# Wide chunks of an attention and feed-forward kernel: three operands of the second layer are built one product earlier, one scaling moves from GpSimd to VectorE, and GpSimd's sums wait

## The chip, the cores and the metric

The kernel runs on one core of a Trainium2 chip. The metric is the device time of one execution in microseconds (us). A core has TensorE (PE in the profile, with its weight loads as PEld), VectorE (DVE), ScalarE (ACT), GpSimd (POOL) and SyncE (SP, which issues DMAs).

## The reference

What is computed, cut to what matters:

```python
kv = np.einsum('bhsd,bhse->bhde', k, v)              # q, k, v: 8 x 8 x 576 x 64
out = np.einsum('bhsd,bhde->bhse', q, kv)
rms = np.sqrt(np.mean(out * out, axis=-1, keepdims=True) + 1e-06)
x = (out / rms * g_norm)                             # as 4608 tokens x 512
h = x @ w_in                                         # w_in: 512 x 2048
g = 0.5 * h * (1.0 + erf(h / sqrt(2)))
y = g @ w_out                                        # w_out: 2048 x 512
```

All arrays are 32-bit floats. A float operand of a matmul is kept as two parts: a high part (the value cast to a shorter type, `fp32r`) and a low part (the value less its high part), and three matmuls, high by high, low by high and high by low, stand for one.

## The kernel before

The tokens are worked in seven chunks. Chunks 0 and 1 (512 tokens each) are plain. Chunks 2 to 6 are wide, with 704, 704, 736, 736 and 704 tokens, and use a Strassen-like scheme: each 2 by 2 block product is made by seven products instead of eight. `FAST` is 2, the first wide chunk, and `NCH` is 7.

**Layer 1 of a wide chunk** is 28 products, `u` = 0 to 27, in four groups of seven (`m` = `u // 7`). Within a group the products come in the order `ORDER = (0, 2, 4, 6, 1, 3, 5)` and write the PSUM bank pairs X, Z, X, Z, Y, Z, Y. A product is 12 matmuls. After each, `Fast.behind` evacuates its bank pair: for product `k` = 0 ScalarE copies (L1205), for 4 ScalarE applies the gelu (L1196), and for 2, 6, 1, 3 and 5 VectorE adds the bank pair to a buffer `e` (L604), after which, for 1, 3 and 5, ScalarE applies the gelu. The bank pair of the last group's product 22 is written again by product 24, that of 24 by 26, and that of 25 by 27, so each of these VectorE adds has to end before the next product but one starts.

**Layer 2** is another 28 products of 12 matmuls ("ticks", table `TICKS`, which begins (0,0), (0,1), (0,2), (2,0), (2,1), (0,3)). An operand of it is made by `Fast.ready`, in two steps: `high`, a cast on ScalarE (L1254), and `low`, a subtraction on VectorE (L1258) that reads two SBUF operands. Operands (0,0), (0,1) and (0,2) are made while layer 1 goes on. Operand (0,3) needs the gelu of product 23; (2,0) and (2,1) need only blocks that were finished long before. Two sums of finished blocks (`Fast.combine`, L1241) run on GpSimd at products 24 and 25 of the last group.

**The next chunk's attention output** is prepared in `within`, beside the products of this chunk. For each of four head pairs `p`, `scale` makes a row of reciprocal norms by a transposition on VectorE (L361) and multiplies it in (L357, two SBUF operands), at products 15, 16, 18 and 20. Then `add_blocks` (L474) forms four sums T3, T1, T2 and T4, all of them on GpSimd.

A chunk without a next one (chunk 6) has neither scalings nor these four sums. In the kernel before, chunk 2 is a special case twice: only there VectorE multiplies the fourth pair (elsewhere GpSimd does), and only there the four sums stand at products 22 to 25 and the first, T3, waits for the `low` of operand (0,2), by `behind(op, latest["low"])`; elsewhere they stand at products 21 to 24 and T3 waits for its inputs alone.

Each engine takes its instructions in the order in which the code issues them; nothing reorders them. In the code, `layer.behind(m, k)` issues the evacuation of the product that was just issued, `within(c, u)` comes after it, and `layer.ready(...)` stood at the end of the loop's body.

Of the kernel before, what the change touches and what calls it, by code (L numbers as in the profile page):

```python
# [23 lines left out]
FAST = PLAIN  # L24
# [15 lines left out]
def linear_attn_rms_gelu_ffn(  # L40
# [18 lines left out]
    nc = tc.nc  # L59
# [3 lines left out]
    B, NP = kv_main.shape[:2]  # L63
# [28 lines left out]
    def pair_of_banks(pool, name):  # L92
        banks[name] = pool.tile([P, 2, 512], F32, name=f"banks_{name}")
# [32 lines left out]
    def block_tile(name, dtype):  # L126
        if name not in home:
            raise KeyError(name)
        width = 2 * WIDEST if name[0] == "d" else 2 * DM
        return home[name].tile([P, width], dtype, name=name)  # L130

    kv_in, late, latest = {}, {}, {}
# [7 lines left out]
    def load_keys(b, p):  # L140

        names["kv", p], t = take()
        main, tail = t[:, :2 * DM], t[:TAIL, 2 * DM:2 * DM + 2 * P]
        nc.sync.dma_start(out=main, in_=kv_main[b, p])
        nc.sync.dma_start(out=tail, in_=kv_tail[b, :, p])
        main, tail = (x.rearrange("p (a n) -> p a n", a=2) for x in (main[:KROWS], tail))
        parts = [main[:, :, j * P:(j + 1) * P] for j in range(NJ)] + [tail]
        kv_in[b, p] = [(x[:, 0], x[:, 1]) for x in parts]
# [409 lines left out]
    GROUPS = NF // 4  # L558
# [155 lines left out]
    def store(acc, t0, to):  # L714
        for t, ps in enumerate(acc):
            nc.scalar.copy(out=to[t], in_=ps)
            nc.sync.dma_start(out=out[t0 + t * P:t0 + (t + 1) * P, :], in_=to[t])
# [143 lines left out]
    for half in range(2):  # L861
# [6 lines left out]
        n = 2 + half  # L868
# [99 lines left out]
    def behind(op, other):  # L968

        tc.add_manual_dep(  # L970
            op.ins, other.ins.name,
            mybir.DependencyInfo(mybir.DependencyClass.Sync, mybir.DependencyReason.DATA),
        )
# [39 lines left out]
    def send():  # L1013

        for x in sent:
            product_out(*x)
        sent.clear()
# [54 lines left out]
    def second_layer(*slots):  # L1072
        c, i = divmod(slots[0], NF)
        if i == 0:
            acc[c] = [bank(f"acc{t}") for t in range(CH // P)]
        layer2(acc[c], [(g.pop(s), s % NF) for s in slots])

    for s in range(PLAIN * NF):
        c, i = divmod(s, NF)
# [43 lines left out]
        else:  # L1123
            spread_matmuls(c, i)
            g[s] = gelu(h.pop(s))
            nxt, k = attn[c + 1], SQUARES.index(i) if i in SQUARES else None
# [184 lines left out]
    def sum_keys(b, ps):  # L1311
        kv_ps[b, 0] = ps
        sum_kv(b, range(NP), ps)
        free.extend(names.pop(("kv", p)) for p in range(NP) if ("kv", p) in names)
        place_kv(b, range(NP))
# [1 line left out]
    SLOTS = 7 * GROUPS  # L1317
    KEYS, QUERIES, DEEPEN = (25, 32, 39, 45), (49, 53), (9, 11)
    SUM, VISITS, NORM = 1, (4, 8), (12, 13)
    SCALE, COMBINE, PIECES = (15, 16, 18, 20), (21, 22, 23, 24), range(31, 52, 3)  # L1320

    def visit(c, u):


        nxt, (a, b) = attn[c + 1], ("ZX" if c == FAST else "WX") if u == VISITS[0] else "WY"
        p = 2 * VISITS.index(u)
        nxt.project_pair(p, a)
        nxt.project_pair(p + 1, b)
        squares.append((p + 1, nxt.square(p + 1)))
        squares.append((p, a))  # L1330

    def within(c, u):

        if c + 3 < B and u in KEYS:
            load_keys(c + 3, KEYS.index(u))
        if c + 2 < NCH and u in QUERIES:
            attn[c + 2].load(QUERIES.index(u))
        if c + 1 == NCH:
            return
        nxt = attn[c + 1]  # L1340
        if c == FAST and u == 0:
            nxt.load(1)
        if c > FAST and u == SUM:
            sum_keys(c + 2, banks["W"][:, 1])
        if c == FAST and u == 2:
            sum_keys(c + 2, banks["Z"][:, 0])
        if u - 1 in VISITS:
            nxt.reduce(*squares.pop(0))
            p, a = squares.pop()
            squares.append((p, nxt.square(p, "w")))  # L1350
        if u - 3 in VISITS:
            nxt.reduce(*squares.pop())
        if u == NORM[0]:
            sums[c] = nxt.fold()
        if u == NORM[1]:
            nxt.inv = nxt.rsqrt(sums.pop(c))
        if u in SCALE:
            p = SCALE.index(u)
            eng = nc.vector if (c, p) == (FAST, NP - 1) else nc.gpsimd
            nxt.scale(p, eng, ("sq", "w")[p % 2])  # L1360
        late = u - (c == FAST)
        if late in COMBINE:
            k = COMBINE.index(late)
            op = nxt.add_blocks(("T3", "T1", "T2", "T4")[k], nc.gpsimd)
            if c == FAST and not k:
                behind(op, latest["low"])
        if u in PIECES:
            nxt.piece(ORDER[PIECES.index(u)])
# [4 lines left out]
    def sum_late(j, place):  # L1373
        names["sums", j], t = take()
        sum_out(j, (place, t[:, :2 * DM]), nc.gpsimd)

    def split_late(u):
        if u in LATE_SPLITS:
            j, h = LATE_SPLITS[u]
            name, t = take(F32R)  # L1380
            at = u if h else u + 1
            lows[at] = high_half(j, h, t[:, :2 * DM])
            split.append((at + 2, name, ("sums", j) if h else None))
        if u in lows:
            low_half(*lows.pop(u))
        if split and split[0][0] == u:
            _, name, whole = split.pop(0)
            for x in sent[:2]:
                product_out(*x)
            del sent[:2]  # L1390
            free.append(name)
            if whole:
                free.append(names.pop(whole))
# [6 lines left out]
    for c in range(FAST, NCH):  # L1400
        layer = Fast(c)
        for u in range(SLOTS):
            m, n = divmod(u, len(ORDER))
            k = ORDER[n]
            layer.product(m, k)
            if (c, u) == (FAST, 1):
                send()
                second_layer(*sorted(g))
                rows_out = [block_tile(n, F32) for n in SPARE[1:]]
                store(acc.pop(c - 1), (c - 1) * CH, [x[:, z * DM:(z + 1) * DM] for x in rows_out for z in range(2)])  # L1410
                acc_banks.release()
                more_banks = tc.alloc_tile_pool(name="more_banks", bufs=1, space=PSUM, reuse_waits="tile")
                for name in "YZ":
                    pair_of_banks(more_banks, name)
            if c + 1 < NCH and u in VISITS:
                visit(c, u)
            layer.behind(m, k)
            if c == FAST and u < 3:
                for j in ((6,), (1, 3), (5,))[u]:
                    attn[c].piece(j)  # L1420
            if c == FAST and u in (3, 6):
                sum_late(*((NJ2 - 2, "x0") if u == 3 else (NJ2 - 1, "x4")))
            within(c, u)
            if c == FAST:
                split_late(u)
            if c == FAST and u in DEEPEN:
                deepen()
            if (c, u) == (FAST, 6):
                low.release()
                last_room = tc.alloc_tile_pool(name="last_room", bufs=1, reuse_waits="tile")  # L1430
                home |= {n: last_room for n in LATE_ROOM}
                free += LATE_ROOM
            if n == 6 and m < GROUPS - 1:
                layer.high(0, m)
            if n == 0 and m:
                layer.low(0, m - 1)
            if n in (3, 4) and m:
                layer.combine((6, 2)[n - 3], m - 1, nc.gpsimd)
            if m == GROUPS - 1 and n > 3:
                layer.ready(*((0, 3), (2, 0), (2, 1))[n - 4])  # L1440
        for k in (6, 2):
            layer.combine(k, GROUPS - 1)
        for i, (k, n) in enumerate(TICKS):
            if i + layer.AHEAD < len(TICKS):
                layer.ready(*TICKS[i + layer.AHEAD])
            if 5 <= i < 5 + GROUPS:
                layer.combine(3, i - 5)
            if 9 <= i < 9 + GROUPS:
                layer.combine(1, i - 9)
            if c < NCH - 1 or i < len(TICKS) - GROUPS:  # L1450
                layer.matmuls(k, n)
                layer.after(k, n)
            within(c, SLOTS + i)
            if c == FAST:
                split_late(SLOTS + i)
        if c == NCH - 1:
            for side in range(2):
                for k, n in TICKS[-GROUPS:]:
                    layer.matmuls(k, n, (side,))
                    layer.after(k, n, (side,))  # L1460
# [61 lines left out]
```

## Time and profile before

| what | us |
| --- | --- |
| three runs: median, lowest, highest | 742.12, 740.96, 743.08 |
| the profiled execution: its own time | 741.02 |
| its span, first to last instruction | 739.2 |
| busy: PE, DVE, ACT, POOL | 732.6, 528.1, 357.3, 122.6 |

The span is 1.8 us shorter than the profiled execution's own time. Rows of the timeline give the start, the duration, the engine, the line of the code, the operation, output and input with sizes, and in brackets how long the engine stood idle just before and what ended that. The duration of a matmul group ends when its last result is modelled to be out, so consecutive groups overlap by 0.16 us; the distance from one start to the next is the time that a product takes. "busy" counts an instruction that is held up after its start as busy.

### The profile page before, as it was taken

The numbers are of one execution on the slowest core, as the hardware profiler recorded it, in microseconds if no ns is written. First come the engines' busy times: TensorE is split into PE (matmuls) and PEld (weight loads), VectorE is DVE, ScalarE is ACT, GpSimd is POOL, SyncE is SP. The second block draws the span as 40 slices with busy tenths as digits, with TensorE's granted clock in tenths as the row PEclk, the third lists the DMA queues.
The fourth block names the chain that finished last, engine by engine and source line by source line (L and its number), as shares of the span: only waits on it lengthen the run. The fifth ranks groups of instructions, "written<-read, shape, count | busy, mean of one in ns | idle before, by whom it ended". The sixth has DMA issues, their size and how long they took to land.

```text
span 739.2 us, 13288 instructions
## 1 busy us (share of the span) xinstructions
PE 732.6 (99%) x5150; PEld 696.3 (94%) x5150; DVE 528.1 (71%) x756; ACT 357.3 (48%) x565; POOL 122.6 (17%) x88
## 2 busy tenths in 40 slices
PE   8999999999999999999999999999999999999998
PEld 6888888888899999999999999999999999999997
DVE  3999998999857689357599257598257598254773
ACT  3788845643465367054365154365154364133640
POOL 1000000000045800013800014600015600022000
PEclk9999999999999999999999999999999999999999
DMA  9998985689998999988999978999978889988893
GB/s 343 407 408 284 364 283 200 220 313 359 346 335 314 361 336 387 408 317 282 323 325 371 406 243 271 313 326 361 395 230 281 276 291 310 335 295 289 295 318 121
DMA packets 84962, 233.66 MB, mean 316 GB/s; under 512 B 8484, under 2 KB 29476, under 8 KB 84900
## 3 DMA queue, kind: packets, MB, share of 16 engines
q1 hardware_dynamic: 84896, 232.82, 88.6%
q8 instruction: 41, 0.67, 0.4%
q14 instruction: 21, 0.17, 0.1%
q10 hardware_dynamic: 4, 0.00, 0.0%
HBM read 193.99 MB, written 38.80 MB: 315 GB/s over the span
## 4 chain that ended last, share of the span: by engine, by line
PE 93%; DMA 3%; DVE 1%; ACT 1%; issue 1%; ACTq 0%; DVEq 0%
PE banks_Z L1276 15%; PE banks_Z L1184 14%; PE acc L708 11%; PE h L676 10%; PE banks_X L1184 10%; PE banks_Y L1184 10%; PE banks_X L1276 10%; PE banks_Y L1276 9%; DMA w_out<-kv_main 1%; DMA w_in<-w_in 1%; PE banks_W L198 1%; PE banks_W L1184 1%; PE banks_W L414 1%; PE a L198 1%; PE banks_W L1276 0%
## 5 line engine op out<-in xcount | busy, mean ns | idle before, releaser
L1258 DVE TENSOR_TENSOR d<-d,d 128x704 fp32r<-128x704 f32 (+1 forms) x140 | 135.3, 988 | 33.8 <-ACT d L1254 33.6
L1254 ACT CAST d<-d 128x704 fp32r<-128x704 f32 (+1 forms) x140 | 105.0, 787 | 25.2 <-DVE d L1241 19.1
L604 DVE TENSOR_TENSOR e<-banks_Z,e 128x704 f32<-128x704 f32 (+1 forms) x53 | 47.7, 900 | 58.3 <-PE banks_Z L1184 46.8
L676 PE MATMUL h<-x,w_in 128*128 128x512 f32 x360 | 82.9, 380 | 0.0
L1276 PE MATMUL banks_X<-d,w_in 128*128 128x352 f32 (+1 forms) x504 | 79.1, 315 | 0.0
L1184 PE MATMUL banks_Z<-d,w_in 128*128 128x352 f32 (+1 forms) x468 | 78.0, 316 | 0.0
L676 PEld LDWEIGHTS h<-x,w_in 128*128 128x128 f32 x360 | 67.8, 189 | 10.1 <-ACT z L631 0.3
L708 PE MATMUL acc<-w_out,gh 128*128 128x512 f32 x256 | 77.0, 382 | 0.1
L1276 PEld LDWEIGHTS banks_X<-d,w_in 128*128 128x128 f32 x504 | 77.1, 189 | 0.0
L1184 PEld LDWEIGHTS banks_Z<-d,w_in 128*128 128x128 f32 x468 | 72.2, 189 | 1.1 <-DVE e L604 0.8
L1241 POOL TENSOR_TENSOR d<-d,d 128x704 f32<-128x704 f32 (+1 forms) x15 | 25.8, 1718 | 284.9 <-ACT d L1196 284.9
L1276 PE MATMUL banks_Y<-d,w_in 128*128 128x352 f32 (+1 forms) x432 | 67.2, 315 | 0.0
L1276 PEld LDWEIGHTS banks_Y<-d,w_in 128*128 128x128 f32 x432 | 66.1, 189 | 0.0
L1184 PE MATMUL banks_X<-d,w_in 128*128 128x352 f32 (+1 forms) x372 | 62.2, 317 | 0.0
L1184 PE MATMUL banks_Y<-d,w_in 128*128 128x352 f32 (+1 forms) x372 | 61.5, 315 | 0.0
L604 DVE TENSOR_TENSOR e<-banks_Y,e 128x704 f32<-128x704 f32 (+1 forms) x30 | 27.0, 903 | 47.4 <-PE banks_Y L1276 28.9
L1276 PE MATMUL banks_Z<-d,d 128*128 128x352 f32 (+1 forms) x360 | 59.8, 315 | 0.1
L1184 PEld LDWEIGHTS banks_X<-d,w_in 128*128 128x128 f32 x372 | 57.4, 189 | 1.4 <-issue 1.0
L1276 PE MATMUL banks_Z<-d,w_in 128*128 128x352 f32 (+1 forms) x360 | 57.9, 315 | 0.0
L1184 PEld LDWEIGHTS banks_Y<-d,w_in 128*128 128x128 f32 x372 | 57.6, 189 | 0.0
L1276 PEld LDWEIGHTS banks_Z<-d,d 128*128 128x128 f32 x360 | 55.8, 189 | 0.4 <-DVE d L1258 0.4
L708 PEld LDWEIGHTS acc<-w_out,gh 128*128 128x128 f32 x256 | 47.9, 189 | 8.5 <-issue 1.4
(228 smaller groups left out, 1129.7 us busy)
## 6 DMA issues: line engine op xcount, KB each, us to landing
w_in<-products_out SPq DMA_DIRECT2D x110, 512.0 KB, 4.8
w_in<-products_in SPq DMA_DIRECT2D x104, 512.0 KB, 4.8
d<-products_in SPq DMA_DIRECT2D x36, 512.0 KB, 5.1
d<-products_out SPq DMA_DIRECT2D x30, 512.0 KB, 4.6
products_in<-w_in SPq DMA_DIRECT2D x36, 256.0 KB, 5.2
w_in<-w_in SPq DMA_DIRECT2D x16, 512.0 KB, 10.2
w_out<-w_out SPq DMA_DIRECT2D x16, 512.0 KB, 10.2
products_out<-w_out SPq DMA_DIRECT2D x32, 256.0 KB, 5.3
```

What stands on the lines that cost most here:

```text
L198: nc.tensor.matmul(out=ps[r, n * D:(n + 1) * D], lhsT=k[:, r], rhs=v[:, r], start=(j == 0), stop=(j == NJ),)
L414: nc.tensor.matmul(out=to[rows(h), :, at], lhsT=kv[b % 2][rows(half), p, h ^ half], rhs=q[rows(half), h, :, at], start=True, stop=True,)
L604: return eng.tensor_tensor(out=out, in0=x, in1=y, op=op)
L676: nc.tensor.matmul(out=h, lhsT=parts["in", i][:, w][:, p * P:(p + 1) * P], rhs=woven(at.x[p][:, x]), start=(m + p == 0), stop=(m == 2 and ...
L708: nc.tensor.matmul(out=ps, lhsT=x[:, ts], rhs=woven(parts["out", i][:, w]), start=(i == 0 and m == 0), stop=(m == 2 and i == NF - 1),)
L1184: nc.tensor.matmul(out=ps[:, n], lhsT=y, rhs=woven(x[:, z, kb]), start=k in (0, 2, 1) and kb + i == 0, stop=kb == 1 and i == 2, skip_group ...
L1241: eng.tensor_tensor(out=out, in0=x, in1=y, op=op)
L1254: nc.scalar.copy(out=t[:, 0], in_=self.source(k, n))
L1258: latest["low"] = nc.vector.tensor_tensor(out=t[:, 1], in0=src, in1=t[:, 0].bitcast(F32), op=ALU.subtract)
L1276: nc.tensor.matmul(out=self.last(k, a) if alone else ps[:, a], lhsT=y, rhs=woven(x[:, z, p]), start=(alone or k in (0, 2, 1)) and n + p + ...
```

## The change

Three edits, in wide chunks:

- `layer.ready` for operands (0,3), (2,0) and (2,1) moves from the end of the loop's body at products 25, 26 and 27 to a place ahead of `layer.behind` at products 24, 25 and 26.
- The fourth pair is multiplied by VectorE in every wide chunk, not only in chunk 2.
- The four sums T3, T1, T2, T4 stand at products 22 to 25 in every wide chunk, and T3 waits for the latest `low` in every one.

```diff
-    SCALE, COMBINE, PIECES = (15, 16, 18, 20), (21, 22, 23, 24), range(31, 52, 3)
+    SCALE, COMBINE, PIECES = (15, 16, 18, 20), (22, 23, 24, 25), range(31, 52, 3)
...
-            eng = nc.vector if (c, p) == (FAST, NP - 1) else nc.gpsimd
+            eng = nc.vector if p == NP - 1 else nc.gpsimd
             nxt.scale(p, eng, ("sq", "w")[p % 2])
-        late = u - (c == FAST)
-        if late in COMBINE:
-            k = COMBINE.index(late)
+        if u in COMBINE:
+            k = COMBINE.index(u)
             op = nxt.add_blocks(("T3", "T1", "T2", "T4")[k], nc.gpsimd)
-            if c == FAST and not k:
+            if not k:
                 behind(op, latest["low"])
...
                 visit(c, u)
+            if m == GROUPS - 1 and 3 <= n < 6:
+                layer.ready(*((0, 3), (2, 0), (2, 1))[n - 3])
             layer.behind(m, k)
...
-            if m == GROUPS - 1 and n > 3:
-                layer.ready(*((0, 3), (2, 0), (2, 1))[n - 4])
```

On VectorE, chunk 3, from the last multiplication's row of norms to the end of layer 1 (`e` and `banks` are evacuations, L1258 the `low` of operands (0,2), (0,3), (2,0) and (2,1) in this order, each with the buffer `d` that it fills):

```order
 L361 STREAM_TRANSPOSE w<-y 128x736
+L357 TENSOR_TENSOR o<-o,w 128x736
 L1258 TENSOR_TENSOR d_3926<-d_3851,d_3926 128x704
-L604 TENSOR_TENSOR e_3959<-banks_Z,e_3941 128x704
-L604 TENSOR_TENSOR e_3993<-banks_Z,e_3941 128x704
-L604 TENSOR_TENSOR e_4011<-banks_Y,e_3993 128x704
-L1258 TENSOR_TENSOR d_4018<-d_3975,d_4018 128x704
+L604 TENSOR_TENSOR e_3957<-banks_Z,e_3941 128x704
+L1258 TENSOR_TENSOR d_3991<-d_3974,d_3991 128x704
+L604 TENSOR_TENSOR e_3994<-banks_Z,e_3941 128x704
+L1258 TENSOR_TENSOR d_4012<-d_3568,d_4012 128x704
+L604 TENSOR_TENSOR e_4015<-banks_Y,e_3994 128x704
```

The first two evacuations of the last group that are to be freed for products 26 and 27 (those of products 24 and 25) now have a `low` ahead of each; before, both came ahead of any of the three. In chunk 2 the same rows moved, but the multiplication (L357) stood there already.

On GpSimd, chunk 3, from the third pair's multiplication to the second block sum (L474 are T3, T1, T2 and T4, L1241 the block sums):

```order
 L357 TENSOR_TENSOR o<-o,sq 128x736
 L1241 TENSOR_TENSOR d_3715<-d_3715 128x704
-L357 TENSOR_TENSOR o<-o,w 128x736
 L474 TENSOR_TENSOR z<-o 128x736
 L474 TENSOR_TENSOR o<-o 128x2x368
 L474 TENSOR_TENSOR w<-z,o 128x736
+L1241 TENSOR_TENSOR d_3851<-d_3852,d_3851 128x704
 L474 TENSOR_TENSOR z<-o,w 128x736
-L1241 TENSOR_TENSOR d_3851<-d_3852,d_3851 128x704
 L1241 TENSOR_TENSOR d_3851<-d_3851 128x704
```

One instruction left GpSimd, and the first block sum now comes ahead of T4, as it did in chunk 2 before.

On ScalarE, chunk 3, the last group (L1196 are gelus, L1254 the casts of operands (0,3), (2,0) and (2,1)):

```order
 L1205 COPY e_3941<-banks_X 128x704
-L1196 ACTIVATE d_3975<-banks_X 128x704
-L1196 ACTIVATE d_3976<-e_4011 128x704
-L1254 CAST d_4018<-d_3975 128x704
+L1196 ACTIVATE d_3974<-banks_X 128x704
+L1254 CAST d_3991<-d_3974 128x704
+L1254 CAST d_4012<-d_3568 128x704
+L1196 ACTIVATE d_3975<-e_4015 128x704
```

The casts of (0,3) and (2,0) now follow the gelu of product 23 at once, ahead of the gelu of product 25.

## Rows read from the trace of the kernel before

**Rows 1.** The page, part 1: TensorE's busy time, share, instructions.

```profile
PE 732.6 (99%) x5150; PEld 696.3 (94%) x5150; DVE 528.1 (71%) x756; ACT 357.3 (48%) x565; POOL 122.6 (17%) x88
```

**Rows 2.** Waits of TensorE's weight loads, 199 to 739: total us, times, longest.

```profile
PEld banks_Z L1184 <- DVE e L604: 0.8, 2, 0.4
PEld banks_Z L1276 <- DVE d L1258: 0.4, 1, 0.4
```

**Rows 3.** Windows, products 24 to 27: length, busy PE, PEld, DVE, ACT, POOL, clock, DMA.

```profile
250.16:257.32 7.16, 7.16 (x50) 7.16 (x49) 2.74 (x3) 2.22 (x3) 7.08 (x6) 1.00 0.92 311
356.46:363.73 7.27, 7.27 (x50) 7.27 (x49) 2.75 (x3) 2.22 (x3) 7.11 (x5) 1.00 0.89 310
464.96:472.44 7.48, 7.48 (x51) 7.48 (x49) 2.89 (x3) 2.30 (x3) 7.32 (x5) 1.00 0.93 299
575.45:582.93 7.48, 7.48 (x51) 7.48 (x50) 2.89 (x3) 2.30 (x3) 7.25 (x6) 1.00 0.89 290
678.25:685.41 7.16, 7.16 (x51) 7.16 (x50) 2.75 (x4) 2.22 (x3) 0.86 (x1) 1.00 0.90 298
```

**Rows 4.** Timeline, chunk 2, last group of layer 1.

```profile
247.55 0.88 DVE L1258 TENSOR_TENSOR d<-d,d 128x704 fp32r<-128x704 f32 x1
248.58 1.68 POOL L474 TENSOR_TENSOR z<-o 128x704 f32<-128x704 f32 x1 [1.95 <-DVE d L1258]
250.34 1.69 POOL L474 TENSOR_TENSOR o<-o 128x704 f32<-128x704 f32 x1
250.43 0.76 ACT L1196 ACTIVATE d<-banks_X 128x704 f32<-128x704 f32 x1 [2.42 <-PE banks_X L1184]
251.98 1.69 POOL L474 TENSOR_TENSOR w<-z,o 128x704 f32<-128x704 f32 x1
253.74 1.95 PE L1184 MATMUL banks_Z<-d,w_in 128*128 128x352 f32 x12
256.36 1.35 DVE L1258 TENSOR_TENSOR d<-d,d 128x704 fp32r<-128x704 f32 x1 [1.52 <-ACT d L1254]
256.92 2.35 POOL L1241 TENSOR_TENSOR d<-d 128x704 f32<-128x704 f32 x1
```

**Rows 5.** Timeline, chunk 3, last group of layer 1 and a tick.

```profile
351.45 1.70 POOL L1241 TENSOR_TENSOR d<-d 128x704 f32<-128x704 f32 x1
352.86 0.77 ACT L1254 CAST d<-d 128x704 fp32r<-128x704 f32 x1
353.09 1.77 POOL L357 TENSOR_TENSOR o<-o,w 128x736 f32<-128x736 f32 x1
353.66 1.95 DVE L1258 TENSOR_TENSOR d<-d,d 128x704 fp32r<-128x704 f32 x1 [0.65 <-ACT d L1254]
355.53 0.88 DVE L604 TENSOR_TENSOR e<-banks_Z,e 128x704 f32<-128x704 f32 x1
356.46 2.06 PE L1184 MATMUL banks_Z<-d,d 128*128 128x352 f32 x12
356.64 0.76 ACT L1196 ACTIVATE d<-banks_X 128x704 f32<-128x704 f32 x1 [2.36 <-PE banks_X L1184]
370.89 2.32 PE L1276 MATMUL banks_Z<-d,d 128*128 128x352 f32 x12
```

**Rows 6.** Timeline, chunk 4: a transposition, the gelu of 23, an evacuation.

```profile
460.39 0.94 DVE L361 STREAM_TRANSPOSE w<-y 128x736 f32<-128x736 f32 x1
465.16 0.78 ACT L1196 ACTIVATE d<-banks_X 128x736 f32<-128x736 f32 x1 [2.49 <-PE banks_X L1184]
467.03 0.93 DVE L604 TENSOR_TENSOR e<-banks_Z,e 128x736 f32<-128x736 f32 x1 [2.25 <-PE banks_Z L1184]
```

**Rows 7.** Timeline, chunk 5: a transposition and the gelu of 23.

```profile
570.88 0.90 DVE L361 STREAM_TRANSPOSE w<-y 128x704 f32<-128x704 f32 x1
575.65 0.78 ACT L1196 ACTIVATE d<-banks_X 128x736 f32<-128x736 f32 x1 [2.49 <-PE banks_X L1184]
```

**Rows 8.** Timeline, chunk 6: the gelu of 23.

```profile
678.45 0.76 ACT L1196 ACTIVATE d<-banks_X 128x704 f32<-128x704 f32 x1 [2.36 <-PE banks_X L1184]
```

## The prediction

> **What bounds the kernel now.** I read the page's busy times first. TensorE is busy for 732.6 of 739.2 us [rows 1], so time is lost or won only where TensorE's products start later or sooner. Next I read whom its queue waits for in the wide chunks: in 540 us it waits 0.8 us, in two waits, for an evacuation that frees bank pair Z, and 0.4 us, once, for the `low` of a layer 2 operand [rows 2]. So no more than about 1 us is to be had here at all, and the question is whether the change makes new waits.
>
> The windows over products 24 to 27 show where to look. A product takes 7.16 / 4 = 1.79 us in the chunks of 704 tokens and 7.48 / 4 = 1.87 us in those of 736; chunk 3 alone took longer, 7.27. VectorE is busy only 2.7 to 2.9 us there. But GpSimd is busy for 7.1 to 7.3 us in chunks 2 to 5, all of the window, and for 0.86 in chunk 6 [rows 3]. In this window, with GpSimd at work without a pause, the three moved operands now fall.
>
> **What a `low` costs beside GpSimd.** A `low` takes 0.88 us when GpSimd is idle (247.55) [rows 4]. In chunk 3 one starts at 353.66 while GpSimd multiplies until 354.86; it ends at 355.61, 0.75 us after GpSimd has ended [rows 5]. Then GpSimd is held: in chunk 2 a `low` ends at 257.71, and the block sum that GpSimd had begun at 256.92, after the `low`, ends at 259.27, 1.56 us later [rows 4]. So a two-operand instruction of VectorE and one of GpSimd exclude each other: who began first finishes, and the other follows with 0.75 us (VectorE) or 1.56 us (GpSimd; scaled by 736/704, 1.63, an estimate). An evacuation, with one operand in PSUM, is not held: the one at 467.03 took its 0.93 [rows 6] beside GpSimd's busy window.
>
> **What an evacuation may cost.** A product can be read 0.20 us after the next one starts: in chunk 6 product 24 starts at 678.25, where the window begins [rows 3], and the gelu of 23 at 678.45 [rows 8]. The product after the next needs the bank pair back. So the add of 24 has 1.79 - 0.20 = 1.59 us for 0.89 us of work, and 0.65 us of slack after 0.05 us for the signal. Chunk 3 shows the price of missing it: with its gelu of 23 at 356.64, product 24 was due at 356.44; the evacuation of 22 ended at 356.41, the product started at 356.46 and took 2.06 us [rows 5] against the usual 1.95 [rows 4]. I count 0.10 for each restart.
>
> **The change, step by step.** With `ready` moved, VectorE's order is: `low` (0,3), evacuation of 24, `low` (2,0), evacuation of 25, `low` (2,1), evacuations of 26 and 27. The first `low` is ready when the gelu of 23 and a cast (0.77 in chunk 3 [rows 5], 0.80 in the wider chunks, the same by size) are done; I take 0.04 us between them and 0.03 us to VectorE, the latter as from 352.86 + 0.77 to 353.66 [rows 5]. The 0.04 no row shows; its bounds are -0.1 (no gap) and 0.08 (GpSimd's T3 to T1, 250.26 to 250.34 [rows 4]), and I take what lies between. A following VectorE instruction starts 0.08 us before the end of the one ahead (355.53 against 355.61).
>
> *Chunk 2.* The gelu ends at 251.19, the `low` is ready at 252.03. GpSimd's T2 begins at 251.98 [rows 4], 0.05 earlier. So T2 runs to 253.67, the `low` to 254.42, the evacuation of 24 to 255.23, and product 26, due at 253.74 [rows 4], starts at 255.28: 1.54 late, 1.64 with the restart. GpSimd's next sum is held to 255.98, so `low` (2,0) ends at 256.73, the evacuation of 25 at 257.54, and product 27, due at 255.28 + 1.89 = 257.17, starts at 257.59: 0.42, with the restart 0.52. Together **2.16 us**. Had the `low` come first: evacuation of 24 at 253.72 in time, T2 to 254.47, `low` (2,0) to 255.22, evacuation of 25 to 256.03, product 27 0.55 + 0.10 late: 0.65.
>
> *Chunk 3.* VectorE now multiplies the fourth pair; it is held by the block sum that ends at 353.15 [rows 5], ends at 353.90, and `low` (0,2), alone, at 354.70. T3 follows 0.15 us behind (248.43 to 248.58 in chunk 2 [rows 4]), and T1 ends two GpSimd sums later, at 354.85 + 1.77 + 0.08 + 1.77 = 358.47. `low` (0,3) is ready at 356.64 + 0.76 + 0.04 + 0.77 + 0.03 = 358.24, ahead of T2. It ends at 359.22, the evacuation of 24 at 360.02; product 26, due at 360.02, starts at 360.07: 0.15 with the restart. T2 to 360.85, `low` (2,0) to 361.60, evacuation of 25 to 362.40, product 27 at 362.45 instead of 361.96: 0.59. Together **0.74**.
>
> *Chunk 4.* Transposition to 461.33 [rows 6], multiplication (0.93, taken as the evacuation's [rows 6]) to 462.30, `low` (0,2) to 463.14, T1 to 466.9, T2 from 466.85. `low` (0,3) is ready at 465.16 + 0.78 [rows 6] + 0.04 + 0.80 + 0.03 = 466.81, 0.04 us before. By the same chain product 26 is in time and 27 loses **0.46**; had T2 come first, 1.66 + 0.51 = 2.17.
>
> *Chunk 5.* Its next chunk is narrower, so GpSimd's sums are shorter: transposition to 571.78 [rows 7], `low` (0,2) to 573.55, T1 to 577.16, T2 from 577.11 to 578.80. `low` (0,3) is ready at 575.65 + 0.78 + 0.87 = 577.30 [rows 7], 0.19 too late: it ends at 579.55, the evacuation of 24 at 580.40, product 26 at 580.45 instead of 579.19 (1.36), and 27 loses another 0.51. Together **1.87**.
>
> *Chunk 6.* GpSimd is idle [rows 3]; `low` (0,3) is ready at 678.45 + 1.60 = 680.05 [rows 8] and ends at 680.93, the evacuation of 24 at 681.74, 0.09 before product 26: **0**.
>
> *Gains.* The late evacuation of product 22 in chunk 3 goes, since the `low` ahead of it is no longer held by GpSimd's multiplication: 0.13. The tick at 370.89, 0.36 us too long [rows 5], goes too. `low` (2,1) and the evacuations of 26 and 27 come 2 us or more before the ticks that need them, so nothing follows there. Together -0.49. The multiplication on VectorE costs nothing by itself: VectorE is idle for more than half of the time [rows 3], and without that cover its 0.9 us would add to the next evacuation. T4 and GpSimd's second block sum, which operand (2,2) waits for, end about where they did, with one instruction less ahead of them and two more holds of 0.75; the tick of (2,2) is six products, over 10 us, behind product 27. The order of the DMAs is the same.
>
> **The sum.** 2.16 + 0.74 + 0.46 + 1.87 - 0.49 = +4.7 us. Against the profiled execution's own 741.0 that is 745.7; the median of the runs shown is 1.1 us above that execution, so 746.8.
>
> **A rule beside it.** The Trainium skill, page "SBUF — State Buffer", section "Who interferes with whom", says that "Issue order, not op shape, decides who blocks." The handover at 256.36 and 256.92 agrees with it [rows 4]. By the rule chunk 2 costs 2.16, and if a waiting VectorE were always let in first, 0.65; no row here has two starts as near as 0.05 us.
>
> **Rivals.** *The first `low` gets in ahead of T2 everywhere.* For it: margins of 0.05, 0.04 and 0.19 us against an unshown 0.04. Against: chunk 5 needs more than the bound of -0.1 gives. Chunks 2 to 5 then lose 0.65, 0.74, 0.46 and some 0.46, less 0.49: +1.8, 743.9. *T2 comes first in chunk 4 too:* 1.71 more, 748.5. *Not slower:* the `low` holds up no evacuation beyond its slack. This is decided by `low` (2,0): it has to end 0.36 to 0.55 us sooner than above in each of chunks 2 to 5, which it does if it doesn't wait for a whole GpSimd sum behind `low` (0,3). For it: VectorE is idle for over half of the window. Against: GpSimd is not [rows 3], and with its next sum always waiting behind a `low`, the next `low` meets it. Then only the gains stay: 741.6.
>
> **How the numbers follow.** What a measurement of this kernel can tell from no change is 0.3%, 2.2 us. The forecast with its neighbours (one of the near ties more or less) has 0.64, all of it slower; the first rival's 743.9 has 0.14, mostly within 0.3%; not slower 0.16, of which faster 0.03 (more than 2.2 us would need gains that no row shows); a loss of more than 7 us 0.06. So faster 0.03, same 0.25, slower 0.72. The range reaches from 743.3, 0.6 below the first rival, to 749.0, 0.5 above the second, for the scatter of the runs.
>
> **What would show it.** In the changed kernel's timeline: `low` (0,3) and (2,0) of 1.6 to 2.4 us in chunks 2 to 5 and 0.9 in chunk 6; waits of TensorE for VectorE's evacuations, about 1.4 us before product 26 in chunks 2 and 5 and about 0.5 us before product 27 in four chunks; windows of products 24 to 27 longer by 0.4 to 2.2 us; the tick of (2,1) in chunk 3 at 1.79. I am wrong if these `low`s run at 0.9, if the gelu of 23 or its cast is ready earlier than I have it, or if GpSimd's sums start later and leave the window free.

## The result

The changed kernel takes 747.61 us (median of six runs, 745.56 to 749.08) against 741.65 us for the kernel before in the same six rounds: a ratio of 1.0081, 95% interval 1.0067 to 1.0095, so 0.8% slower. Its profiled execution took 745.97 us with a span of 744.0 us, 4.8 us more than the span before. One execution of the first experiment below ran at a mean granted clock of 0.655 and took 1096.7 us; it counts in that run's median but not in its ratio.

The page, part 1, of the changed kernel:

```profile
PE 734.2 (99%) x5150; PEld 696.3 (94%) x5150; DVE 532.7 (72%) x759; ACT 358.1 (48%) x565; POOL 119.9 (16%) x85
```

Read beside [rows 1], TensorE's work is as it was (the weight loads are busy for the same 696.3 us), and its share still reads 99%. Of the 4.8 us, only 1.6 show there, as busy time of its matmuls (734.2 us for 732.6). The 4.8 us are found in the waits of its weight loads from 199 to 746 us (total us, times, longest):

```profile
PEld banks_Z L1184 <- DVE e L604: 4.0, 5, 1.6
PEld banks_Y L1184 <- DVE e L604: 2.1, 4, 0.6
```

Before, it was 0.8 for bank pair Z, nothing for Y, and 0.4 for a layer 2 operand [rows 2]. That last wait is gone. What was added is all for evacuations (L604) by VectorE. The windows over products 24 to 27 of chunks 2 to 6, with length and busy times in the columns of [rows 3]:

```profile
250.06:259.35 9.29, 7.69 (x51) 7.15 (x49) 5.91 (x5) 3.67 (x5) 9.21 (x6) 1.00 0.93 306
358.46:366.39 7.93, 7.63 (x51) 7.16 (x49) 4.61 (x5) 3.68 (x5) 7.85 (x5) 1.00 0.92 305
467.26:475.29 8.03, 7.78 (x50) 7.45 (x49) 4.60 (x5) 3.81 (x5) 7.95 (x5) 1.00 0.87 288
578.29:587.65 9.36, 8.01 (x50) 7.45 (x49) 5.92 (x5) 3.81 (x5) 9.35 (x5) 1.00 0.81 259
682.97:690.21 7.24, 7.24 (x51) 7.17 (x49) 3.91 (x5) 3.67 (x5) 0.87 (x1) 1.00 0.84 294
```

Four undisturbed products take 7.16 or 7.48 us. The windows are longer than that by 2.13, 0.77, 0.55, 1.88 and 0.08, together 5.4 us. VectorE's busy time doubles in chunks 2 and 5, though it gained only two instructions in the window (three before [rows 3], five now), which alone take under 1 us each; the rest is `low`s that stand and are counted as busy. Chunk 2's timeline shows it:

```profile
250.31 0.76 ACT L1196 ACTIVATE d<-banks_X 128x704 f32<-128x704 f32 x1 [2.42 <-PE banks_X L1184]
251.10 1.46 ACT L1254 CAST d<-d 128x704 fp32r<-128x704 f32 x2
251.88 1.69 POOL L474 TENSOR_TENSOR w<-z,o 128x704 f32<-128x704 f32 x1
251.92 2.40 DVE L1258 TENSOR_TENSOR d<-d,d 128x704 fp32r<-128x704 f32 x1 [2.49 <-ACT d L1254]
253.53 2.32 POOL L1241 TENSOR_TENSOR d<-d,d 128x704 f32<-128x704 f32 x1
254.24 0.88 DVE L604 TENSOR_TENSOR e<-banks_Z,e 128x704 f32<-128x704 f32 x1
255.04 1.56 DVE L1258 TENSOR_TENSOR d<-d,d 128x704 fp32r<-128x704 f32 x1
255.17 2.06 PE L1184 MATMUL banks_Z<-d,w_in 128*128 128x352 f32 x12 [1.37 <-DVE e L604]
256.52 0.88 DVE L604 TENSOR_TENSOR e<-banks_Y,e 128x704 f32<-128x704 f32 x1
257.45 2.06 PE L1184 MATMUL banks_Y<-d,d 128*128 128x352 f32 x12 [0.23 <-DVE e L604]
```

T2 (L474, at 251.88) begins 0.04 us before the `low` of (0,3). The `low` stands until T2 ends, at 253.57, and takes 2.40 us instead of 0.88. The evacuation of product 24, due at 252.04, waits behind it until 254.24, and product 26 starts at 255.17 instead of 253.64. The next `low` stands behind GpSimd's block sum (L1241) until 255.85, and product 27 is late once more.

### The profile page after: what moved, and what is told of

It reads as the page before. It is cut to its first block, busy times and chain, and to the rows that moved or that the text cites. A ratio compares the mean times of both kernels' runs of the same rounds, so it can differ in the third digit from the quotient of the medians.

```text
span 744.0 us, 13282 instructions
## 1 busy us (share of the span) xinstructions
PE 734.2 (99%) x5150; PEld 696.3 (94%) x5150; DVE 532.7 (72%) x759; ACT 358.1 (48%) x565; POOL 119.9 (16%) x85
## 4 chain that ended last, share of the span: by engine, by line
PE 92%; DMA 4%; DVE 2%; ACT 1%; issue 1%; DVEq 0%; ACTq 0%
PE banks_Z L1276 15%; PE banks_Z L1184 13%; PE acc L708 11%; PE banks_X L1276 10%; PE h L676 10%; PE banks_X L1184 10%; PE banks_Y L1184 9%; PE banks_Y L1276 9%; DMA w_out<-kv_main 1%; DMA d<-products_out 1%; DMA w_in<-w_in 1%; PE banks_W L198 1%; PE banks_W L1184 1%; PE banks_W L414 1%; DVE e L604 1%
## 5 line engine op out<-in xcount | busy, mean ns | idle before, releaser
L1258 DVE TENSOR_TENSOR d<-d,d 128x704 fp32r<-128x704 f32 (+1 forms) x140 | 137.7, 1006 | 39.2 <-ACT d L1254 39.0
L1254 ACT CAST d<-d 128x704 fp32r<-128x704 f32 (+1 forms) x140 | 105.0, 788 | 18.7 <-DVE d L1241 9.1
L604 DVE TENSOR_TENSOR e<-banks_Z,e 128x704 f32<-128x704 f32 (+1 forms) x53 | 47.7, 901 | 49.1 <-PE banks_Z L1184 33.1
L1241 POOL TENSOR_TENSOR d<-d,d 128x704 f32<-128x704 f32 (+1 forms) x15 | 28.4, 1890 | 287.7 <-ACT d L1196 287.7
L604 DVE TENSOR_TENSOR e<-banks_Y,e 128x704 f32<-128x704 f32 (+1 forms) x30 | 27.0, 902 | 47.2 <-PE banks_Y L1276 33.2
```

What stands on the lines that cost most here:

```text
L604: return eng.tensor_tensor(out=out, in0=x, in1=y, op=op)
L1241: eng.tensor_tensor(out=out, in0=x, in1=y, op=op)
L1254: nc.scalar.copy(out=t[:, 0], in_=self.source(k, n))
L1258: latest["low"] = nc.vector.tensor_tensor(out=t[:, 1], in0=src, in1=t[:, 0].bitcast(F32), op=ALU.subtract)
```

## The experiments

All runs with a ratio are against the kernel before on the same chip.

**The three operands back where they were; the other two parts stay.**

```diff
-            if m == GROUPS - 1 and 3 <= n < 6:
-                layer.ready(*((0, 3), (2, 0), (2, 1))[n - 3])
             layer.behind(m, k)
...
+            if m == GROUPS - 1 and n > 3:
+                layer.ready(*((0, 3), (2, 0), (2, 1))[n - 4])
```

> The changed kernel with the three operands made where they stood before (products 25 to 27, behind the evacuations); VectorE's multiplication and GpSimd's waiting sums stay. My theory (a low ahead of an evacuation is held by GpSimd's sums): no wait of TensorE at products 26 and 27 in any chunk, product 24 of chunk 3 on time; span 0.1 to 0.5 us under the kernel before. Rival (the sums at 22 to 25, or the multiplication on VectorE, cost the time): 2 us or more over the kernel before.

Measured: 740.58 us, ratio 0.9995 (0.9986 to 1.0005), span 738.6. The waits of the weight loads from 199 to 746 us, the one row for bank pair Z, with none for Y and none for a layer 2 operand:

```profile
PEld banks_Z L1184 <- DVE e L604: 0.8, 2, 0.4
```

All five windows are at 7.16 or 7.48 us. So VectorE's multiplication and the waiting sums, tried here together, cost nothing; by the spans of the profiled executions they win 0.6 us, which is within the scatter of the runs.

**Only the three operands moved, in the kernel before.**

```diff
+            if m == GROUPS - 1 and 3 <= n < 6:
+                layer.ready(*((0, 3), (2, 0), (2, 1))[n - 3])
             layer.behind(m, k)
...
-            if m == GROUPS - 1 and n > 3:
-                layer.ready(*((0, 3), (2, 0), (2, 1))[n - 4])
```

> The kernel before with only the three operands moved. My theory, by the same chains with T3 one product earlier in chunks 3 to 5: chunk 2 as in the changed kernel (2.1 us), chunk 3 about 0.6 before product 26 and 0.6 before 27, chunk 4 0.55 and 0.5, chunk 5 0.3 and 0.5; less the tick of chunk 3, 0.4; together +4.8 us (between 3.5 and 5.5). Rival (the three parts cost only together, because T3's wait moves GpSimd's sums into the way): under +2.5 us.

Measured: 745.83 us, ratio 1.0069 (1.0052 to 1.0086), span 743.6. Its windows over products 24 to 27:

```profile
249.84:259.12 9.28, 7.69 (x51) 7.16 (x50) 5.90 (x5) 3.68 (x5) 9.20 (x6) 1.00 0.93 329
358.25:366.70 8.45, 7.79 (x49) 7.26 (x49) 5.14 (x5) 3.68 (x5) 8.29 (x5) 1.00 0.90 292
467.57:476.07 8.50, 8.02 (x51) 7.46 (x49) 5.06 (x5) 3.81 (x5) 8.34 (x5) 1.00 0.88 296
579.07:587.24 8.17, 7.98 (x50) 7.45 (x49) 4.74 (x5) 3.81 (x5) 8.01 (x5) 1.00 0.84 289
```

Longer by 2.12, 1.29, 1.02 and 0.69 in chunks 2 to 5: the pattern worked out beforehand for sums that start one product earlier, chunk by chunk. The move by itself costs the time, and the other parts only decide in which chunk a `low` meets which sum.

**The four sums at products 27 to 30**, so that the two `low`s find GpSimd idle.

```diff
-    SCALE, COMBINE, PIECES = (15, 16, 18, 20), (22, 23, 24, 25), range(31, 52, 3)
+    SCALE, COMBINE, PIECES = (15, 16, 18, 20), (27, 28, 29, 30), range(31, 52, 3)
```

> The changed kernel with T3, T1, T2 and T4 at products 27 to 30 instead of 22 to 25, so that GpSimd is idle when the lows of (0,3) and (2,0) come. My theory: these lows take 0.9 us in every chunk, no wait of TensorE at products 26 and 27, span 0.2 to 0.6 us under the kernel before, unless the sums now hold lows of layer 2 beyond their lead. Rival (the place ahead of the evacuations costs by itself): waits of about 0.5 us and more at products 26 or 27 stay in four or five chunks, +2 us or more.

Measured: 743.51 us, ratio 1.0036 (1.0024 to 1.0048), span 741.4. The expected gain did not come. The waits before 26 and 27 did go, but product 24 now starts 0.54 to 0.68 us late in each of chunks 2 to 5. Chunk 2's timeline:

```profile
246.49 2.40 POOL L1241 TENSOR_TENSOR d<-d,d 128x704 f32<-128x704 f32 x1
247.27 2.38 DVE L1258 TENSOR_TENSOR d<-d,d 128x704 fp32r<-128x704 f32 x1
249.57 0.88 DVE L604 TENSOR_TENSOR e<-banks_Z,e 128x704 f32<-128x704 f32 x1
250.50 2.06 PE L1184 MATMUL banks_Z<-d,d 128*128 128x352 f32 x12 [0.45 <-DVE e L604]
251.75 0.89 DVE L1258 TENSOR_TENSOR d<-d,d 128x704 fp32r<-128x704 f32 x1 [1.30 <-ACT d L1254]
```

The `low` of (0,3) takes 0.89, as expected. But with the four sums out of the queue ahead of them, GpSimd's block sums (L1241) came forward to 246.49 and held the `low` of (0,2), the one ahead of the evacuation of product 22. I had not looked at what stands next in GpSimd's queue. It is the same mechanism two products earlier.

**The same (sums at 27 to 30), with the first block sum also waiting for the `low` of (0,2).**

```diff
-            eng.tensor_tensor(out=out, in0=x, in1=y, op=op)
+            return eng.tensor_tensor(out=out, in0=x, in1=y, op=op)
...
             if n == 0 and m:
                 layer.low(0, m - 1)
+                latest["first"] = latest["low"]
             if n in (3, 4) and m:
-                layer.combine((6, 2)[n - 3], m - 1, nc.gpsimd)
+                op = layer.combine((6, 2)[n - 3], m - 1, nc.gpsimd)
+                if n == 3 and m == GROUPS - 1:
+                    behind(op, latest["first"])
```

> The run with the sums at products 27 to 30, in which the first block sum on GpSimd also waits for the low of (0,2), so that it can no longer hold that low and with it the evacuation of product 22. All three operands still stand ahead of the evacuations. My theory: no wait of TensorE at products 24, 26 or 27 in any chunk; the first two lows 0.9 us; span 0.2 to 0.6 us under the kernel before. Rival (the place ahead of the evacuations costs even when GpSimd is out of the way): 0.3 us or more before 26 or 27 in several chunks, +1 us or more.

Measured: 740.69 us, ratio 0.9997 (0.9988 to 1.0007), span 738.6. Chunk 2's timeline:

```profile
251.54 0.89 DVE L1258 TENSOR_TENSOR d<-d,d 128x704 fp32r<-128x704 f32 x1 [2.49 <-ACT d L1254]
253.15 0.88 DVE L1258 TENSOR_TENSOR d<-d,d 128x704 fp32r<-128x704 f32 x1
253.29 2.06 PE L1184 MATMUL banks_Z<-d,w_in 128*128 128x352 f32 x12
```

All three operands stand ahead of the evacuations here, as in the change, and product 26 loses only its restart: the window is 7.29 us long instead of 9.29, and the other four are 7.23 to 7.52. The place alone costs 0.03 to 0.13 us a chunk; with GpSimd's instructions in the way it was up to 2.13.

**The three operands at the same products, but behind the evacuations.**

```diff
-            if m == GROUPS - 1 and 3 <= n < 6:
-                layer.ready(*((0, 3), (2, 0), (2, 1))[n - 3])
             layer.behind(m, k)
+            if m == GROUPS - 1 and 3 <= n < 6:
+                layer.ready(*((0, 3), (2, 0), (2, 1))[n - 3])
```

> The changed kernel with each of the three operands made at the same product (24, 25, 26), but behind that product's evacuation. My theory: the lows are still held by GpSimd (1.6 to 2.4 us), but the evacuation of 24 goes ahead of them and that of 25 ends 0.05 to 0.6 us before product 27 is due: no wait, or one of 0.1 us in chunk 3; span 0.3 to 0.5 us under the kernel before. Rival (making them a product sooner costs, wherever in the slot): 2 us or more over the kernel before.

Measured: 740.60 us, ratio 0.9997 (0.9988 to 1.0006), span 739.5 in the profiled execution, which was one of the two longest of ten. Chunk 2's timeline:

```profile
252.58 1.69 POOL L474 TENSOR_TENSOR w<-z,o 128x704 f32<-128x704 f32 x1
252.76 0.89 DVE L604 TENSOR_TENSOR e<-banks_Z,e 128x704 f32<-128x704 f32 x1 [2.62 <-PE banks_Z L1184]
253.56 1.46 DVE L1258 TENSOR_TENSOR d<-d,d 128x704 fp32r<-128x704 f32 x1
254.95 0.88 DVE L604 TENSOR_TENSOR e<-banks_Y,e 128x704 f32<-128x704 f32 x1
256.13 1.95 PE L1184 MATMUL banks_Y<-d,d 128*128 128x352 f32 x12
```

The `low` is held (1.46), the evacuation behind it ends at 255.83, and product 27 starts on time at 256.13. The other windows are at 7.16 or 7.48 us too, but for a single restart of 0.11 in chunk 3, as expected. Being made a product sooner costs next to nothing; being ahead of the evacuation does.

**Only (0,3) ahead of its evacuation.**

```diff
-            if m == GROUPS - 1 and 3 <= n < 6:
-                layer.ready(*((0, 3), (2, 0), (2, 1))[n - 3])
+            if m == GROUPS - 1 and n == 3:
+                layer.ready(0, 3)
             layer.behind(m, k)
+            if m == GROUPS - 1 and 4 <= n < 6:
+                layer.ready(2, n - 4)
```

> The changed kernel with only operand (0,3) ahead of its evacuation (product 24); (2,0) and (2,1) stay at 25 and 26, behind the evacuations. My theory: the waits before product 26 stay as in the changed kernel's profile (1.53 in chunk 2, 0.10 in 3, none in 4, 1.26 in 5, and 0.1 for each restart), those of 0.4 to 0.5 before product 27 go; span 2.4 to 2.9 us over the kernel before. Rival (the waits before 27 only follow from those before 26, or are owed to something else than the place of the second low): waits of 0.3 us and more before 27 stay, over +4 us, or those before 26 go too, under +1 us.

Measured: 744.67 us, ratio 1.0046 (1.0029 to 1.0062), span 743.7. Waits of TensorE's matmuls, 199 to 746 us:

```profile
PE banks_Z L1184 <- DVE e L604: 3.8, 3, 1.4
```

In the changed kernel they are:

```profile
PE banks_Z L1184 <- DVE e L604: 2.5, 2, 1.4
PE banks_Y L1184 <- DVE e L604: 1.0, 4, 0.3
```

Those for Y, before product 27, are gone here, so they belong to the second `low`. Those before 26 stayed, and chunk 4 has one too, which the changed kernel's profile did not have (its window is 9.13 us long, 1.65 over an undisturbed one): that is why the span is 4.5 us over that of the kernel before and not 2.4 to 2.9. By the size of the span alone the rival would have been met; the place of the waits decides against it. Two of its four executions had spans of 741.6 and 741.7, the other two 743.7 and 743.8.

**The changed kernel again, twice.**

> The changed kernel itself once more, on this chip. If the starts of T2 and of the low of (0,3), 0.04 us apart in chunk 2 and 4, fall the same way in every execution: waits of 1.5 and 1.3 us before product 26 in chunks 2 and 5 alone, +4.8 us. If they fall differently: a wait before 26 in chunk 4 (+1.6), or none in chunk 2 (-1.5).

> The changed kernel for one more look, with the same two ways: the first low of chunk 2 held and that of chunk 4 not, as in the profile shown, and +4.8 us over the kernel before; or another pattern, with 1.6 us more or less.

Measured: 746.64 us, ratio 1.0076 (1.0057 to 1.0094), and a single execution of 747.44; the profiled spans are 745.3 and 745.6. Chunk 4's timeline, first of the changed kernel's profile shown above, then of the two further profiled executions:

```profile
469.11 0.93 DVE L1258 TENSOR_TENSOR d<-d,d 128x736 fp32r<-128x736 f32 x1 [2.53 <-ACT d L1254]
469.12 2.52 POOL L474 TENSOR_TENSOR w<-z,o 128x736 f32<-128x736 f32 x1
```

```profile
468.83 1.76 POOL L474 TENSOR_TENSOR w<-z,o 128x736 f32<-128x736 f32 x1
468.84 2.54 DVE L1258 TENSOR_TENSOR d<-d,d 128x736 fp32r<-128x736 f32 x1 [2.53 <-ACT d L1254]
472.26 2.14 PE L1184 MATMUL banks_Z<-d,w_in 128*128 128x368 f32 x12 [1.38 <-DVE e L604]
```

```profile
469.04 2.56 DVE L1258 TENSOR_TENSOR d<-d,d 128x736 fp32r<-128x736 f32 x1 [2.53 <-ACT d L1254]
469.05 1.76 POOL L474 TENSOR_TENSOR w<-z,o 128x736 f32<-128x736 f32 x1
```

In the first the `low` runs at once and T2 is held (2.52); in the other two T2 runs and the `low` is held, and the window of chunk 4 is 9.64 and 9.66 us long instead of 8.03. Chunk 2 and chunk 5 fell the same way in all three. So the near tie of chunk 4 is decided anew in each execution, at a price of 1.6 us.

**Each of the four sums as two instructions of half the columns.**

```diff
-            return eng.tensor_tensor(out=t, in0=a, in1=b, op=op)
+            first, rest = (
+                eng.tensor_tensor(out=t[:, n], in0=a[:, n], in1=b[:, n], op=op) for n in range(2)
+            )
+            return first
```

> The changed kernel with each of the four sums issued as two GpSimd instructions of half the columns, all else the same. My theory: a low waits for what is left of one GpSimd instruction, so with instructions of about 0.85 us the first low ends at most 0.8 us later than alone, and the second mostly inside the slack: before product 26 waits of 0 to 0.8 us per chunk, before 27 none or up to 0.2; +0.3 to +2.2 us over the kernel before. Rival (each handover between GpSimd and VectorE has a price of its own, whatever the length): twice as many handovers, the waits before 27 stay at 0.4 or more, +4 us or more.

Measured: 741.82 us, ratio 1.0013 (1.0004 to 1.0023), span 739.5. Chunk 2's timeline (L1261 is the `low`, L475 the half sums):

```profile
251.31 0.92 DVE L1261 TENSOR_TENSOR d<-d,d 128x704 fp32r<-128x704 f32 x1 [2.49 <-ACT d L1257]
251.44 3.19 POOL L475 TENSOR_TENSOR w<-z,o 128x352 f32<-128x352 f32 x2
252.95 0.88 DVE L1261 TENSOR_TENSOR d<-d,d 128x704 fp32r<-128x704 f32 x1
253.08 2.06 PE L1187 MATMUL banks_Z<-d,w_in 128*128 128x352 f32 x12
```

The same work on GpSimd at the same place, in shorter pieces, and the second `low` (252.95) is hardly held: a half sum is over by the time VectorE has evacuated. No wait for bank pair Y, before 27, is left in any chunk; by the windows chunk 3 still loses 0.37 us and chunk 5 0.80, before 26, and the others 0.16 or less. So what costs is the length of one GpSimd instruction, not the number of handovers.

## Why the prediction was right

**Bound.** As predicted, nothing but TensorE's waits moved the time: 6.1 us of waits of weight loads for evacuations against 0.8 before, and 0.4 for a `low` that went.

**What a `low` costs beside GpSimd.** Right: the two held `low`s of chunk 2 end 0.75 us after GpSimd does (253.57 to 254.32, 255.85 to 256.60).

**The chains, chunk by chunk**, from the windows of the profiled execution:

| chunk | predicted, us | measured, us |
| --- | --- | --- |
| 2 | 2.16 | 2.13 |
| 3 | 0.74 | 0.77 |
| 4 | 0.46 | 0.55 |
| 5 | 1.87 | 1.88 |
| 6 | 0 | 0.08 |

The gap of 0.04 us between the gelu and its cast, which no row showed, was 0.03 (250.31 + 0.76 to 251.10). The gains of 0.49 came: chunk 3's product 24 is on time and its long tick is back at 1.79 us. The sum of the table less the gains is 4.9, and the span grew by 4.8.

**The slack of an evacuation** was counted to the wrong point, and chunk 6 shows it. Four rows of its timeline:

```profile
684.77 0.89 DVE L1258 TENSOR_TENSOR d<-d,d 128x704 fp32r<-128x704 f32 x1 [1.97 <-ACT d L1254]
685.58 0.88 DVE L604 TENSOR_TENSOR e<-banks_Z,e 128x704 f32<-128x704 f32 x1
686.52 1.79 PEld L1184 LDWEIGHTS banks_Z<-d,w_in 128*128 128x128 f32 x12
686.55 2.03 PE L1184 MATMUL banks_Z<-d,w_in 128*128 128x352 f32 x12
```

Its `low` was not held, as predicted, and product 26 began on time, 3.58 us after product 24; but it took 2.03 us for 1.95. The evacuation ended at 686.46, 0.09 us before the product as predicted, and product 26's weight load began only 0.03 us ahead of its matmuls, where product 25's led by 0.14. So the evacuation is due at the weight load, and the slack was 0.14 us less than the 0.65 that I counted to the matmuls. The run with the sums at 27 to 30 and the waiting block sum agrees: in its chunks 3 to 6 the `low`s are not held, the weight load of product 26 leads by 0.03 to 0.07, and the windows are 0.03 to 0.08 longer.

**A sign that did not hold.** I named `low`s of (0,3) of 1.6 to 2.4 us in all of chunks 2 to 5. In the profile that fits the forecast they took 2.40, 1.02, 0.93 and 2.26. My own chains had chunks 3 and 4 at about 0.9 to 1.0, so the list of signs contradicted them, and the chains were right.

**The near ties.** I gave the forecast to chunk 2 lost and chunk 4 won. The first held in each of three profiles; the second held in one of three. All eleven executions of the changed kernel fall into two groups: four of 745.6 to 746.0 us, at the 745.7 that the sum gave for one execution, and seven of 747.4 us and more (three of these, 748.5 to 749.1, also have a mean granted clock of 0.997). That would be why the medians are 6.0 us apart and not 4.7. So part of the agreement is luck. The profiled execution happened to be one of the faster group; the forecast of 746.8 for the median is near 747.61 also because the kernel before had its median 0.5 us lower in these rounds than the 742.12 that I added to; and in chunk 2 a margin of 0.05 us was decided on a gap of 0.04 that no row showed. The second rival, T2 first in chunk 4 too, at 748.5 by the median, was no rival but a second outcome of the same kernel: where it occurred, chunk 4 lost 2.16 and 2.18 us, and I had worked out 2.17. I had given it a place in the range, not in the predicted value.

**The rule beside it.** The Trainium skill, page "SBUF — State Buffer", section "Who interferes with whom", says that issue order decides who blocks. In chunk 2 the trace agrees at a distance of 0.04 us: T2, at 251.88, blocks the `low` of 251.92. In chunk 4 the recorded starts can't tell any more: in one execution the `low` is recorded 0.01 us ahead and wins, in another it is recorded 0.01 us ahead and is held.

**The rivals.** That the first `low` gets in ahead of T2 everywhere did not happen in any of the three profiles. That the `low`s would cost nothing was refuted where GpSimd has its full sums in the window, and is nearly what the runs show when they are out of it and the block sum waits, or when they are halved.

**Left open.** Which of the executions behind the medians lost chunk 4's tie was not seen, since only the profiled ones have rows; the two groups of times agree with the price, but that is argued, not shown.

## What to carry to other kernels

An operand that is made earlier on an engine with spare time is not free if it goes ahead of the instruction that releases the next buffer: ask what may hold it there, and not only how long it takes. In these runs a VectorE subtraction with two SBUF operands waited for the elementwise GpSimd instruction that was running (2.40 us for 0.88), and everything behind it on VectorE waited too. Behind the evacuations it cost next to nothing, and with GpSimd's sums cut in halves at most 0.80 us a chunk. When work is taken out of a queue, look at what moves up in it.

## What the runs showed of the hardware that was not expected

One program had two times, 1.6 us apart in one window, because two engines began 0.01 us apart and either could go first; the profile of one execution shows only one of the two, and the recorded starts do not tell which. And in this kernel a bank pair had to be free by the next product's weight load, 0.14 us ahead of its matmuls: where the load led by 0.03 us only, the product took 2.03 us for 1.95, though its matmuls began on time.
